# Head of a spectral-mixing block with its gradients: turned copies of grad_out and of the spectrum by DMA, the gate on w_down, inverse written in rows

## The chip, the cores and the metric

The kernel runs on one core of one Trainium2 chip. The core has five engines with a queue of instructions each: TensorE (PE, whose weight loads the profile lists as PEld), VectorE (DVE), ScalarE (ACT), GpSimd (POOL) and SyncE (SP, which issues most of the DMAs). Each engine takes its instructions in the order of its queue and waits on semaphores for what others make. The metric is the time of one execution on the device, in microseconds (us); lower is better.

## The reference

A block of a network with a modulated (adaLN) spectral filter and a modulated bilinear feed-forward part is run forward, and its gradients with respect to all inputs but one are formed for a given `grad_out`. x and grad_out are 1 x 2048 x 576 in bfloat16; w_gate and w_up are 576 x 4608, w_down 4608 x 576, w_mod 576 x 3456. Cut to what matters:

```python
mod = silu(c) @ w_mod                      # six vectors of 576: sa, ca, ga, sb, cb, gb
h = layernorm(x) * (1 + ca) + sa
x = x + ga * irfft2(rfft2(h) * (w_r + 1j * w_i))
h = layernorm(x) * (1 + cb) + sb
out = x + gb * (((h @ w_gate) * (h @ w_up)) @ w_down)
out, vjp = jax.vjp(f, A_x, A_w_r, A_w_i, B_w_gate, B_w_up, B_w_down, c, w_mod)
return out, *vjp(grad_out)
```

The gradient that reaches the hidden layer is `(gb * grad_out) @ w_down.T`. It does not depend on the forward pass, except on the vector gb.

## The kernel before, in words

The 2048 tokens lie on 128 partitions as 16 tiles (`NT`), token p*16+t in tile t. The 2-D Fourier transform is done by matmuls with tables: along the 576 columns to 289 frequencies (padded to 292, `FP`), then along the tokens in two steps, 16 x 128, with the twiddles in the tables. The frequencies are worked on in 73 groups of 4 (`NG`), and these in 19 chunks of 4 groups (`NCH`). F = 4608 is cut into 36 blocks of 128 (`NFB`).

The kernel has a head, a main loop over the 36 blocks (forward and gradient products of the feed-forward part: gup on line 581, u8p on line 607, u57p on line 526), and a tail (the way back through the norms and the filter). The change is in the head, which has these parts:

- The modulation vectors. `mod_load` (237) loads a sixth of w_mod, `mod_make` (243) multiplies and spreads it over all partitions as `modh[j]`, with the evacuation on DVE, and stores it. MSA comes first, then MCA; MGB (the gate gb) is made after the first `s1_cols`, the other three after stage 1.
- Stage 1, a software pipeline over 16 tiles: `s1_norm` (280) normalises a tile, modulates it and turns it on PE (trp), `s1_cols` (302) multiplies with the table RD (zp, evacuated into zt: the first half by ACT, the second by DVE), `s1_rows` (313) with G1 (vp) and writes the spectrum `VA`. x is loaded four tiles at a time by `x_load` (256), with the statistics of all four in one call of `norm_stats`.
- Stage 2, a pipeline over 19 chunks: `s2_turn` (343) turns four 128x128 blocks of VA on PE and ACT copies them out as VT; `s2_filter` (351) multiplies with BD2 (xp), ACT writes Xc, DVE multiplies with the filter (fm) and forms Yg; `s2_back` (369) turns Yg on PE, and DVE writes YT; `s2_inv` (377) multiplies with BDA (ap_), and ACT writes the result over the same columns of VA, with each frequency's 32 values (c, a) next to one another.
- Stage 3, a pipeline over 16 tiles: `s3_rows` (395) reads VA as weights, 128 frequencies with a stride of 32 elements, and goes back along the tokens; `s3_cols` (407) goes back along the columns with IR; `s3_norm` (421) forms x1 and the modulated h2, and every fourth tile's h2 is turned by a DMA into h2T (444).
- The product of the hidden gradient, called u4 (449 to 477): each tile of grad_out (gon) is multiplied by the gate on DVE (452) and turned on PE, five blocks a tile, into goT (458). Then w_down is loaded in 18 pairs of blocks (466), each pair is turned by a DMA into wdT (467; two buffers), and 720 matmuls of 128x512 (475) make ghhT, which is evacuated as ghh_st (two buffers; the first nine blocks on DVE, the rest by turns on ACT and DVE) and stored to DRAM (477). The main loop reads it from there.

u4 stands last in the program, but the compiler's scheduler writes one order for each engine and fills PE's gaps in stages 1 to 3 with u4's matmuls. `issue_after(x)` lets a DMA be issued only after instruction x; `high_priority` draws instructions forward. Within a queue nothing overtakes. SP's queue holds nearly all loads, all turns by DMA and the stores of the head. The tiles come from pools; a pool with n buffers makes the n+1st tile wait for the last reader of the first.

The gon product is used twice more: as the weights of u57p in the main loop, and as the rows of an output.

Of the kernel before, what the change touches and what calls it, by code (L numbers as in the profile page):

```python
# [82 lines left out]
def build(ctx, tc, A_x, A_w_r, A_w_i, B_w_gate, B_w_up, B_w_down, c_in, w_mod, grad_out,  # L83
# [39 lines left out]
    ones_f = glob.tile([128, 128], FP32, name="ones_f")  # L123
    nc.vector.memset(ones_f[:], 1.0)

    pick = glob.tile([128, 2, 128], BF, name="pick")
    nc.vector.memset(pick[:], 0.0)
    for q in range(2):
        nc.vector.memset(pick[:, q, 64 * q:64 * q + 64], 1.0)


# [11 lines left out]
    def norm_stats(xt, pool, nt, name, rstd_out):  # L143

        st = pool.tile([128, nt, 2, nc.vector.BN_STATS_DIM], FP32, name=name + "_st")
        mv = pool.tile([128, nt, nc.vector.BN_AGGR_DIM], FP32, name=name + "_mv")
        for t in range(nt):
            for h in range(2):
                nc.vector.bn_stats(out=st[:, t, h, :], in_=xt[:, t, h * 288:(h + 1) * 288])
            nc.vector.bn_aggr(out=mv[:, t, :], in_=st[:, t, :, :])  # L150
        nc.scalar.activation(out=rstd_out, in_=mv[:, :, 1], func=ACT.Sqrt, bias=eps_t[:], scale=1.0)
        nc.vector.reciprocal(out=rstd_out, in_=rstd_out)
        nmr = pool.tile([128, nt], FP32, name=name + "_nmr")
        nc.vector.scalar_tensor_tensor(out=nmr[:], in0=mv[:, :, 0], scalar=-1.0, in1=rstd_out, op0=MUL, op1=MUL)
        return nmr
# [28 lines left out]
    gonf = res2.tile([128, NT * D + 64], BF, name="gon")  # L184
    gon = gonf[:, 0:NT * D].rearrange("p (t d) -> p t d", t=NT)

    with ExitStack() as hs:
# [13 lines left out]
        r2 = hs.enter_context(ExitStack())  # L201
        r1 = r2.enter_context(ExitStack())
        wn = pool("hwn", 1, "right", stack=r2).tile([128, 2, NT, FP], BF, name="wn")
        hw2 = pool("hc1", 2, "right", stack=r1)
        modh = [hp1.tile([128, D], BF, name="modh%d" % j) for j in range(6)]
# [4 lines left out]
        nc.gpsimd.memset(gonf[:, NT * D:NT * D + 64], 0.0)  # L210
# [4 lines left out]
        c_bf = hp1.tile([128, 5], BF, name="c_bf")  # L215
        nc.vector.memset(c_bf[:], 0.0)
        with nc.allow_non_contiguous_dma(reason="tiny c load"):
# [25 lines left out]
        def mod_make(j, wm):  # L243
            for h in range(2):
# [5 lines left out]
                else:  # L250
                    evac(modh[j][:, h * 288:(h + 1) * 288], ps[:, 0:288], eng="v")
# [4 lines left out]
        def x_load(c4):  # L256
            xt = hw2.tile([128, 4, D], BF, name="xt", bufs=3)
            nc.sync.dma_start(xt[:], x_v[:, 4 * c4:4 * c4 + 4, :])
            xts.append(xt)

        wms = {MSA: mod_load(MSA)}
        x_load(0)
        wms[MCA] = mod_load(MCA)
        T = {"RD": load_table(hp1, "RD", "tA")}
        T["G1"] = load_table(hp1, "G1", "tB")
        first = mod_make(MSA, wms[MSA])
        mod_make(MCA, wms[MCA])
        with tc.issue_after(first):
            x_load(1)
            wms[MGB] = mod_load(MGB)  # L270
            nc.sync.dma_start(gon, go_v)
# [5 lines left out]
        Vv = VA[:].rearrange("k (g t c f) -> k g t c f", g=NG, t=NT, c=2)  # L277
        hTs, zts, n1s = {}, {}, {}

        def s1_norm(t):  # L280
            c4, tt = t // 4, t % 4
            if tt == 0:
# [4 lines left out]
                n1s["nmr"] = norm_stats(xts[c4], hw2, 4, "ln1", rstd1g[:, t:t + 4])  # L287
            n1 = n1s[c4]
            nc.scalar.activation(out=n1[:, tt, :], in_=xts[c4][:, tt, :], func=ACT.Identity, bias=n1s["nmr"][:, tt:tt + 1], scale=rstd1g[:, t:t + 1])
            nm = hw2.tile([128, D], BF, name="nm")  # L290
# [11 lines left out]
        def s1_cols(t):  # L302
            zt = zts[t] = hw2.tile([128, 2, FP], BF, name="zt", bufs=3)
            for cc in range(2):
# [3 lines left out]
                evac(zt[:, cc, :], zp[:, :FP], eng=("a" if cc == 0 else "v"))  # L308
            if t == 0:
                with tc.issue_after(mm.ins):  # L310
                    mod_make(MGB, wms[MGB])

# [21 lines left out]
        r1.close()  # L334
        with ExitStack() as rc:
            c2 = pool("hc2", 2, "right", stack=rc)
            VTs, Ygs, YTs = {}, {}, {}
# [5 lines left out]
            def s2_turn(ci):  # L343
                g0, ng, f0, w = dims(ci)
                pt = fps.tile([128, 4, 128], BF, name="trv", tag="fp")
                for j in range(ng):
                    nc.tensor.transpose(pt[:, j, :], VA[:, (g0 + j) * 128:(g0 + j + 1) * 128], ident[:])
                VT = VTs[ci] = c2.tile([128, 4, 128], BF, name="VT")
                evac(VT[:, 0:ng, :], pt[:, 0:ng, :], eng="a")

            def s2_filter(ci):
                g0, ng, f0, w = dims(ci)
                xp = fps.tile([128, 4, 128], FP32, name="xp", tag="fp")
                for j in range(ng):
                    nc.tensor.matmul(xp[:, j, :], lhsT=VTs[ci][:, j, :], rhs=T["BD2"][:], start=True, stop=True)
# [21 lines left out]
            def s2_inv(ci):  # L377
# [4 lines left out]
                Ac = VA[:, g0 * 128:(g0 + ng) * 128].rearrange("k (j f e) -> k j e f", f=4, e=2 * NT)  # L382
                evac(Ac, ap_[:, 0:ng, :].rearrange("k j (e f) -> k j e f", f=4), eng="a")

            pipeline(NCH, [s2_turn, s2_filter, s2_back, s2_inv])
            T["GB"] = load_table(hp1, "GB", "tB")
            T["IR"] = load_table(hp1, "IR", "tA")
        r2.close()
# [3 lines left out]
        Av = VA[:].rearrange("k (f c a) -> k f c a", c=2, a=NT)  # L392
        uts, ybs = {}, {}

        def s3_rows(sa):
# [3 lines left out]
            for fc in range(3):  # L399
                f0 = FS[fc]  # L400
                o = upa[:, fc, :] if fc < 2 else upb[:, 0, :]
                nc.tensor.matmul(o, lhsT=Av[:, f0:f0 + 128, 0, sa], rhs=T["GB"][:, sa, 1:3, :].rearrange("k v s -> k (v s)"), start=True, stop=False)
                nc.tensor.matmul(o, lhsT=Av[:, f0:f0 + 128, 1, sa], rhs=T["GB"][:, sa, 0:2, :].rearrange("k v s -> k (v s)"), start=False, stop=True)
# [724 lines left out]
```

## Time and profile before

| | us |
|---|---|
| median of three runs | 1632.08 |
| lowest and highest | 1628.67, 1633.07 |
| the profiled execution | 1636.95 |
| its span (first to last instruction) | 1635.2 |
| its head, up to the first gup matmul | 293.5 |
| PE busy | 1566.0 |
| DVE busy | 1007.8 |
| ACT busy | 567.6 |
| mean granted PE clock | 0.987 of full |

The profile comes from one execution recorded by the hardware. A view of it gives busy time by engine; groups of instructions by source line, with `out<-in` the names of the tiles; the idle time ahead of them and what ended it ("releaser"); and a timeline. L475 is line 475 of the kernel. A row on SP marked SPq is the time that its queue took to issue a DMA, not the time of the transfer; the time to its landing is listed separately.

### The profile page before, as it was taken

What the parts mean: (1) busy time and instruction counts of PE and PEld (TensorE: products, weight loads), DVE (VectorE), ACT (ScalarE), POOL (GpSimd) and SP (SyncE); (2) the same over time, 40 slices, a digit from 0 to 9 for tenths busy, and PEclk for the clock granted to TensorE, in tenths of its full rate; (3) what the DMA queues carried; (4) which work ended last, traced back from release to release, by engine and by line L of the source; (5) the groups of instructions that cost most, each with busy time, mean ns of one, the idle gap of its engine ahead of it and who ended that gap; (6) DMA issues with size and microseconds to landing.
All of it is one profiled execution on the core that took longest, in us unless ns stands there. A gap on an engine that the chain in (4) does not pass through costs nothing.

```text
span 1635.2 us, 29989 instructions
## 1 busy us (share of the span) xinstructions
PE 1566.0 (96%) x11354; PEld 1066.1 (65%) x11354; DVE 1007.8 (62%) x2642; ACT 567.6 (35%) x1056; POOL 161.3 (10%) x266
## 2 busy tenths in 40 slices
PE   6999999999999999999999999999999879899997
PEld 4645544566767676666767676666766656677765
DVE  7878733566564747565564747565564764678645
ACT  5697522322222222222222222222222355565022
POOL 0101100101000010101010010101000001100232
PEclk9999999999999999999999999999999989999998
DMA  9866976586768586776767686876757786636674
GB/s 349 289 183 196 267 214 192 148 162 123 145 134 165 114 170 121 158 147 114 161 129 153 135 161 117 161 135 142 158 103 136 190 240 202 231 97 193 254 216 151
DMA packets 482242, 280.35 MB, mean 171 GB/s; under 512 B 404753, under 2 KB 449426, under 8 KB 481202
## 3 DMA queue, kind: packets, MB, share of 16 engines
q1 hardware_dynamic: 462098, 204.26, 55.1%
q0 software_dynamic: 20000, 74.19, 15.5%
q8 instruction: 88, 1.44, 0.4%
q14 instruction: 56, 0.46, 0.1%
HBM read 108.51 MB, written 82.31 MB: 117 GB/s over the span
## 4 chain that ended last, share of the span: by engine, by line
PE 74%; DMA 6%; DVE 4%; issue 2%; ACT 2%; SPq 0%; POOL 0%; ACTq 0%; DVEq 0%; POOLq 0%
PE u57p L526 25%; PE gup L581 19%; PE u8p L607 17%; PE u4p L475 6%; PE u3p L1028 3%; DMA Xn<-xn_d 2%; DMA n2c<-n_d 2%; DMA wdB<-in_B_w_down_dram 1%; PE yp L937 1%; DMA out_dram<-o 1%; PE zp L801 1%; DVE gwt L849 0%; ACT u L956 0%; DMA x1t<-x_d 0%; DVE fm L167 0%
## 5 line engine op out<-in xcount | busy, mean ns | idle before, releaser
L612 DVE TENSOR_TENSOR acc<-acc,u8p 128x288 f32<-128x288 f32 x1088 | 429.4, 450 | 352.5 <-PE u8p L607 351.2
L581 PE MATMUL gup<-h2T,wgu 128*128 128x512 bf16 x1440 | 433.1, 379 | 0.0
L607 PE MATMUL u8p<-wT,ggT 128*128 128x288 bf16 x1152 | 314.7, 286 | 4.4 <-DVE acc L612 4.4
L607 PE MATMUL u8p<-wT,guT 128*128 128x288 bf16 x1152 | 314.7, 286 | 0.0
L581 PEld LDWEIGHTS <-wgu 128*128 128x128 bf16 x1440 | 140.8, 98 | 96.7
L528 ACT CAST so<-u57p 128x288 bf16<-128x288 f32 x216 | 86.2, 399 | 326.9 <-PE u57p L526 325.0
L607 PEld LDWEIGHTS <-guT 128*128 128x128 bf16 x1152 | 112.8, 98 | 101.5 <-issue 4.8
L475 PE MATMUL u4p<-goT,wdT 128*128 128x512 bf16 x720 | 165.0, 379 | 1.4 <-ACT ghh_st L139 1.4
L582 ACT CAST gT<-gup 128x512 bf16<-128x512 f32 x144 | 84.4, 586 | 226.6 <-PE gup L581 226.6
L526 PE MATMUL u57p<-gon,hh_sf 128*128 128x288 bf16 x1152 | 150.0, 287 | 0.0
L582 ACT CAST uT<-gup 128x512 bf16<-128x512 f32 x144 | 84.4, 586 | 188.5 <-PE gup L581 186.7
L526 PE MATMUL u57p<-h2p,gu_sf 128*128 128x288 bf16 x1152 | 148.8, 286 | 0.0
L526 PE MATMUL u57p<-h2p,gg_sf 128*128 128x288 bf16 x1152 | 148.2, 286 | 0.0
L1028 PEld LDWEIGHTS <-hl 128*128 128x128 bf16 x1152 | 112.9, 99 | 41.0 <-issue 11.3
L526 PEld LDWEIGHTS <-hh_sf 128*128 128x128 bf16 x1152 | 113.1, 98 | 35.1
L607 PEld LDWEIGHTS <-ggT 128*128 128x128 bf16 x1152 | 112.9, 98 | 29.0
L526 PEld LDWEIGHTS <-gu_sf 128*128 128x128 bf16 x1152 | 112.7, 98 | 28.4
L526 PEld LDWEIGHTS <-gg_sf 128*128 128x128 bf16 x1152 | 112.5, 98 | 28.3
L475 PEld LDWEIGHTS <-wdT 128*128 128x128 bf16 x720 | 69.2, 98 | 74.7 <-issue 1.9
L141 DVE CAST ghh_st<-u4p 128x512 bf16<-128x512 f32 x90 | 61.8, 687 | 67.7 <-PE u4p L475 64.7
L1028 PE MATMUL u3p<-wdB,hl 128*128 128x288 bf16 x672 | 96.4, 291 | 6.6 <-DMA wdB<-in_B_w_down_dram 5.8
L586 POOL DMA_DIRECT2D hhT_d<-hhT x36 | 33.2, 922 | 602.4 <-DVE hhT L583 598.7
(355 smaller groups left out, 1682.6 us busy)
## 6 DMA issues: line engine op xcount, KB each, us to landing
ghhT_d<-ghh_st SPq DMA_DIRECT2D x36, 512.0 KB, 3.3
ghh<-ghhT_d POOLq DMA_DIRECT2D x36, 512.0 KB, 7.7
hhT_d<-hhT POOLq DMA_DIRECT2D x36, 512.0 KB, 6.6
hl<-hhT_d SPq DMA_DIRECT2D x32, 576.0 KB, 7.9
out_dram<-woT SPq DMA_DIRECT2D x72, 128.0 KB, 2.0
wdn<-in_B_w_down_dram SPq DMA_DIRECT2D x18, 288.0 KB, 3.4
out_dram<-so SPq DMA_DIRECT2D x36, 144.0 KB, 2.4
wgu<-in_B_w_up_dram POOLq DMA_DIRECT2D x18, 256.0 KB, 5.3
```

What stands on the lines that cost most here:

```text
L141: nc.vector.tensor_copy(dst, src)
L475: nc.tensor.matmul(pt[:], lhsT=wdT[:, j, m, :], rhs=goT[:, 4 * sb4:4 * sb4 + 4, m, :], start=(m == 0), stop=(m == 4))
L526: mm = nc.tensor.matmul(pw[:, 0:288], lhsT=sf[:, t, :], rhs=rhs_n[:, t, h * 288:(h + 1) * 288], start=(t == 0), stop=(t == NT - 1))
L528: nc.scalar.copy(so[:, h * 288:(h + 1) * 288], pw[:, 0:288])
L581: nc.tensor.matmul(pt[:], lhsT=wgu[:, wi_, m, jw * 128:(jw + 1) * 128], rhs=h2T[:, ts_, m, :], start=(m == 0), stop=(m == 4))
L582: nc.scalar.copy(dstT[:, ts_, :], pt[:])
L586: nc.gpsimd.dma_start(hhT_d[:, :, fb, :].rearrange("tp f x -> f tp x"), hhT[:].rearrange("f (tp ti) p -> f tp (ti p)", ti=2))
L607: nc.tensor.matmul(pu[:, 0:288], lhsT=l_, rhs=r_, start=(k == 0), stop=(k == len(mms) - 1))
L612: nc.vector.tensor_tensor(out=dst, in0=dst, in1=pu[:, 0:288], op=ADD)
L801: nc.tensor.matmul(zp[:, :FP], lhsT=gyTs[t][:, m, :], rhs=T["RD"][:, m, cc, :], start=(m == 0), stop=(m == 4))
L937: nc.tensor.matmul(yp[:, 0:288], lhsT=ut[:, fc, cc * 128:(cc + 1) * 128], rhs=T["IR"][:, fc, cc, h * 288:(h + 1) * 288], start=(k == 0), s ...
L1028: mm = nc.tensor.matmul(p2[:, 0:288], lhsT=hls[fb // 9][:, fb % 9, ti * 128:(ti + 1) * 128], rhs=(wdA[:, fb] if fb < 15 else wdB[:, fb - 1 ...
```

## The change

- grad_out is not multiplied before it is turned. Four DMA turns of four tiles each (20 blocks of 128x128) make goT straight from the loaded grad_out, issued in the stage 1 code after the first `s1_cols`; the 80 PE transposes and 16 evacuations go. The gate is put on w_down's pairs, on DVE, after their load and ahead of their turn. gon is still multiplied by the gate for its later uses, but after the last h2.
- `s2_turn` goes. Five DMA turns (16, 16, 16, 16 and 9 blocks) make one VT of all of VA between stages 1 and 2, issued after the turn of w_down's fourth pair. Stage 2 is a pipeline of three steps.
- w_down's pairs are loaded and turned up to seven pairs ahead (two buffers of one pool and five of another): pairs 0 and 1 in stage 1, 2 and 3 after it, 4 to 6 after the VT turns, then one for each pair used.
- `s2_inv` writes VA as rows: for each c and a, all frequencies next to one another. `s3_rows` reads its 128 frequencies without a stride.
- Start: x's first tile is loaded and normalised alone, then tiles 2 to 4; MCA is made before MSA, MSA's evacuation is on ACT; the load of c is drawn forward.
- Evacuations: the second half of zt goes to ACT for odd tiles; ghh_st of the first nine blocks goes from DVE to ACT.
- Constants ones_f and pick are made in the tail, on POOL. The tables GB and IR are loaded after the VT turns.

The diff, cut to its core:

```diff
-                n1s["nmr"] = norm_stats(xts[c4], hw2, 4, "ln1", rstd1g[:, t:t + 4])
+            if t == 0 or tt == (1 if c4 == 0 else 0):
+                n = 1 if t == 0 else 4 - tt
+                nmr = norm_stats(xts[c4][:, tt:tt + n, :], hw2, n, "ln1", rstd1g[:, t:t + n], 4)
...
-        first = mod_make(MSA, wms[MSA])
         mod_make(MCA, wms[MCA])
+        first = mod_make(MSA, wms[MSA], "a")
...
+        def turn_pair(k):
+            f0 = k * FB4
+            wdT = wdTs[k] = (u4w if k % 7 < 2 else u4r[0]).tile([128, FB4, 5, 128], BF, name="wdT")
+            wdn = wdn2[:, k % 2, :, :]
+            with tc.issue_after(first):
+                nc.sync.dma_start(wdn[:, :, 0:D], B_w_down[f0 * 128:(f0 + FB4) * 128, :].rearrange("(j f) d -> f j d", f=128))
+            nc.vector.tensor_tensor(out=wdn[:, :, 0:D], in0=wdn[:, :, 0:D], in1=modh[MGB][:].unsqueeze(1).to_broadcast([128, FB4, D]), op=MUL)
+            turns.append(nc.sync.dma_start_transpose(out=wdT[:].rearrange("q j m f -> q (j m) f"), in_=wdn.rearrange("f j d -> f (j d)")).ins)
...
-                evac(zt[:, cc, :], zp[:, :FP], eng=("a" if cc == 0 else "v"))
+                evac(zt[:, cc, :], zp[:, :FP], eng=("a" if cc == 0 or t % 2 else "v"))
             if t == 0:
                 with tc.issue_after(mm.ins):
                     mod_make(MGB, wms[MGB])
+                for k in range(2):
+                    turn_pair(k)
+                    for t0 in (8 * k, 8 * k + 4):
+                        nc.sync.dma_start_transpose(out=goT[:, t0:t0 + 4, :, :].rearrange("q t m p -> q (t m) p"), in_=gon[:, t0:t0 + 4, :].rearrange("p t d -> p (t d)"))
...
+        u4r = [pool("u4r", 5, "right")]
+        for k in range(2, 4):
+            turn_pair(k)
...
+            VT = pool("hvt", 1, "right", stack=rc).tile([128, NG, 128], BF, name="VT")
+            for g0 in range(0, NG, 16):
+                g1 = min(g0 + 16, NG)
+                with tc.issue_after(turns[3]):
+                    vt_made = nc.sync.dma_start_transpose(out=VT[:, g0:g1, :], in_=VA[:, g0 * 128:g1 * 128]).ins
+            for k in range(4, 7):
+                turn_pair(k)
...
-            def s2_turn(ci):
...
-                Ac = VA[:, g0 * 128:(g0 + ng) * 128].rearrange("k (j f e) -> k j e f", f=4, e=2 * NT)
+                Ac = VA[:].rearrange("k (e f) -> k e f", f=FP)[:, :, f0:f0 + w].rearrange("k e (j f) -> k j e f", f=4)
...
-            pipeline(NCH, [s2_turn, s2_filter, s2_back, s2_inv])
+            pipeline(NCH, [s2_filter, s2_back, s2_inv])
...
-                nc.tensor.matmul(o, lhsT=Av[:, f0:f0 + 128, 0, sa], rhs=T["GB"][:, sa, 1:3, :].rearrange("k v s -> k (v s)"), start=True, stop=False)
+                nc.tensor.matmul(o, lhsT=Av[:, 0, sa, f0:f0 + 128], rhs=T["GB"][:, sa, 1:3, :].rearrange("k v s -> k (v s)"), start=True, stop=False)
...
-                nc.vector.tensor_tensor(out=gon[:, t, :], in0=gon[:, t, :], in1=modh[MGB][:], op=MUL)
...
-                nc.tensor.transpose(pt[:, m, :], gonf[:, t * D + m * 128:t * D + (m + 1) * 128], ident[:])
-            evac(goT[:, t, :, :], pt[:])
...
-                    evac(st[:, 4 * sb4:4 * sb4 + 4, :], pt[:], eng=("v" if fb < 9 else None))
+                    evac(st[:, 4 * sb4:4 * sb4 + 4, :], pt[:], eng=("a" if fb < 9 else None))
...
+            if fb0 // FB4 + 7 < NFB // FB4:
+                turn_pair(fb0 // FB4 + 7)
+        with tc.issue_after(h2_made[-1]):
+            for t in range(NT):
+                nc.vector.tensor_tensor(out=gon[:, t, 0:D], in0=gon[:, t, 0:D], in1=modh[MGB][:], op=MUL)
```

## The prediction

> **What bounds the kernel now.** I read the share of each engine first, then the span in 40 slices. TensorE is busy in nine tenths or more of nearly every slice; the slices that are not full are the first and a few in the tail.
>
> ```profile
> PE   6999999999999999999999999999999879899997
> ACT  5697522322222222222222222222222355565022
> ```
>
> The change touches the head alone (before the first gup matmul at 293.5 us), about the first seven slices. There PE looks as full as elsewhere, but in the head its fullness says little: the product of w_down and grad_out (line 475) is filler, put wherever PE would idle. So I cut the head at its own borders and asked for busy time in each stretch. Columns: stretch, length, busy time and count of PE, weight loads, DVE, ACT, POOL, then granted clock, DMA share, GB/s.
>
> ```profile
> 22.30:63.80 41.50, 37.92 (x345) 27.22 (x344) 37.27 (x109) 32.58 (x66) 2.13 (x4) 1.00 0.92 304
> 63.80:71.20 7.40, 6.50 (x63) 4.89 (x61) 4.11 (x9) 2.32 (x4) 0.00 (x0) 1.00 0.98 342
> 71.20:132.50 61.30, 56.00 (x461) 30.31 (x459) 48.60 (x131) 57.81 (x56) 5.16 (x9) 1.00 0.64 198
> 132.50:186.50 54.00, 49.96 (x351) 34.09 (x351) 45.90 (x136) 35.84 (x74) 10.81 (x20) 1.00 0.82 230
> 186.50:293.50 107.00, 105.65 (x490) 47.74 (x489) 38.73 (x66) 31.94 (x55) 2.47 (x5) 1.00 0.75 213
> ```
>
> These are stage 1 (its first 22 us left out), the gap before the chunks, the 19 chunks of stage 2, stage 3, and the rest of the filler. In the chunks ACT is the fullest (57.81 of 61.30); the same view of line 475 alone puts 167 filler matmuls (42.28 us) there, 62 in stage 3 and 488 in the last stretch. So every piece of a stage that gets shorter saves nothing by itself: the filler not done in it is done after stage 3, at 0.216 us a matmul (405 of them in 87.57 us in one row of the timeline). What counts is when stage 3 ends, and how much filler is left then.
>
> The timeline shows one chunk, from one transpose of Yg to the next, 2.76 us (start, length, engine, line; the mean pace over 19 chunks is 61.3/19 = 3.2):
>
> ```profile
> 81.45 0.40 PE L373 MATMUL try__1011<-ident,Yg 128*128 128x128 bf16 x4 [0.17 <-DVE Yg L367]
> 81.69 0.39 PE L355 MATMUL xp<-T_BD,VT 128*128 128x128 bf16 x4
> ...
> 82.11 0.71 ACT L139 CAST Xc<-xp 128x512 bf16<-128x512 f32 x1
> ...
> 82.70 0.61 ACT L139 COPY VT<-trv 128x512 bf16<-128x512 bf16 x1
> ...
> 82.86 0.76 DVE L167 TENSOR_TENSOR fm<-Xc,wn 128x512 bf16<-128x512 bf16 x2 [0.53 <-ACT Xc L139]
> ...
> 83.17 2.46 ACT L139 CAST VA<-ap__1039 128x512 bf16<-128x512 f32 x1
> ...
> 83.86 0.29 DVE L367 TENSOR_TENSOR Yg<-fm 128x256 bf16<-128x256 bf16 x1
> ...
> 84.21 0.40 PE L373 MATMUL try__1045<-ident,Yg 128*128 128x128 bf16 x4 [0.18 <-DVE Yg L367]
> ```
>
> ACT needs 0.7 + 0.6 + 2.5 = 3.8 us at its longest; but the chain xp, Xc, fm, Yg, transpose alone takes 2.6 to 2.8 us with ACT prompt, as here, since each chunk's Yg comes behind the last one's.
>
> **The change, part by part.** The order in which each engine gets its instructions is fixed; I compared it before and after. In the main loop PE's order is the same; the tail differs in some 150 places without a new wait. I take both at zero, give or take 2.
>
> *PE transposes removed:* 73 of VA and 80 of grad_out. At spacings of 0.057 (four in 0.23 us) and 0.065 us (15 in about 1.0) that is 9 us of PE work. It is a gain only where PE does not idle instead.
>
> *Turns by DMA.* In their place come 4 turns of 20 blocks (grad_out) and 5 of 73 blocks in all (VA). What SP needs to issue one, in the rows of before:
>
> ```profile
> 44.78 7.99 SPq L467 DMA_TRANSPOSE wdT<-wdn  x2
> 153.39 3.06 SPq L444 DMA_TRANSPOSE h2T<-h2p  x1
> 375.44 2.25 SPq L591 DMA_TRANSPOSE gu_sf<-guT  x1
> 377.78 7.32 SPq L591 DMA_TRANSPOSE hh_sf<-hhT  x1
> 385.16 2.19 SPq L591 DMA_TRANSPOSE gg_sf<-ggT  x1
> ```
>
> These are 20, 20, 16, 16 and 16 blocks: 0.4, 0.15, 0.14, 0.46 and 0.14 us a block. Three stacked turns (48 blocks) land in 8.6 to 11.9 us, 0.18 to 0.25 a block. I take 0.18, and 0.136 and 0.4 as ends.
>
> *Stage 1.* In SP's new order the load of the last four x tiles stands behind 4 turns of grad_out and 2 of w_down (100 blocks), the first of which waits for grad_out (issued at 14.20, 12.7 us to landing: 26.9) and issues near 29. Before, the same x load was issued at 23.42 and landed 7.3 us later. Now: 29 + 100 x 0.18 = 47, landed about 52; DVE needs it at 45.3 by the pace of before. Stage 1 ends **6 us** later (2.5 at 0.136 a block, 12 at 0.25 and up; -2 if DVE, which loses 16 casts of zt to ACT at 0.46 each, makes the stage shorter and the load is in time). The loads of wr and wi, and of the last mod vectors, stand behind it as well. The split of x's first tile starts transposes some 1.5 us earlier, but MGB's matmuls still wait for their weights: 0.
>
> *Gap and stage 2.* The VA turns wait for the fourth w_down turn, which stands behind the modb stores, and those behind the mod evacuation. Before, that was done 8.0 us after stage 1's end; with a store and a turn issued after it I put the first VA turn at 9.8. ACT's first write into VA (chunk 0's inverse) must wait for all five turns, since they read all of VA, and it stands in ACT's queue ahead of the Xc of chunk 3: so the chunks can't pass the third until the last turn has landed, 73 x 0.18 + 1.8 = 15 (12 to 20) after the first's issue. From there 16 chunks at 2.7: ACT has lost VT (0.66) and writes VA in rows of f, for which the nearest rows are the tail's contiguous writes of A, median 0.603 and 0.586, against 2.43 to 2.60; so the chain of 2.6 to 2.8 binds, not ACT. With 3 us of drain: 9.8 + 15 + 16 x 2.7 + 3 = 71 against 68.7 from stage 1's end to the last chunk before (63.8 to 132.5): **+2.3** (-3 to +11). So the ACT relief, 19 x 0.5 = 9.5, is real and is eaten by the wait for VT; if that cover were gone the stage would gain it.
>
> *Idle PE and its clock.* While VA is turned PE has only 49 fillers (10.6 us) in some 25 us, and for chunks 1 to 8 none, since the next evacuation of filler stands on ACT behind chunk 9: its buffer waits for a store that stands deep in SP's queue. Before, an idle of 4.39 us on PE in the tail was followed by a clock of 0.76:
>
> ```profile
> 1399.74 1.12 PE L1028 MATMUL u3p<-wdB,hl 128*128 128x288 bf16 x4 [4.39 <-DMA wdB<-in_B_w_down_dram]
> ```
>
> and in the 10 us window after it the granted clock was 0.76, with four 128x128 matmuls at 0.107 apart rather than 0.057. **+2** (0, when the chain hides it, to 4.5). The Trainium skill, "TensorE: Matmul & The Clock Gate", section "HAM oscillation — how this bites in real kernels", has a rule that speaks against such a change: an idle window of about 3.4 us halves PE's clock and some 3.4 us of steady work brings it back; by it, chunks with PE a quarter busy might stay at half clock throughout, and 16 chunks with some 12 matmuls each at 0.05 us more would cost about 10 us (an estimate). The row shows the drop, but not how long a thin load holds it.
>
> *Stage 3 and the rest.* Stage 3 holds 56 fillers in place of 62 and does not begin behind a 2.5 us write of VA: **-2** (0 to -4). 513 fillers are left behind it in place of 488: 25 x 0.216 = **+5.4**. The gon multiplications move behind h2 on DVE (16 x 0.447), and two of DVE's evacuations may queue behind a burst: **+0.5** (0 to 1); ghh_st of the first nine blocks on ACT (0.586 rather than 0.687) covers the rest, as does u4p's buffering. The gate's product on a pair of w_down, not in the trace, is some 2 x 0.447 = 0.9 us on DVE by gon's row; DVE is busy 38.73 us of the last 107, which hides 11 of the 18, and the two in stage 1 stand ahead of its zt casts, at 1.8 if nothing covers them, which the x wait does. The memsets moved to the tail run on POOL (10% busy): 0.
>
> Sum: 6 + 2.3 + 2 - 2 + 5.4 + 0.5 = **+14** on the profiled execution's 1636.95 (span 1635.2), so 1651 for such an execution; against the median, 1632.1 + 14 = **1646**. That execution is 0.3% over the median, about what a measurement of this kernel can tell from no change.
>
> **The rivals.** (a) *The turns are hidden and PE work counts.* If the DMA turns land before anyone needs them and the filler fills the gaps, the 9 us of transposes is all that is left: 1632 - 9 = 1623, and up to 1627 by the terms below. For it: PE is 96% busy. Against it: VA can't be turned before stage 1 ends, and only 49 fillers stand there. It decides if the last VA turn lands within 16 us of stage 1's end, for then stage 2 is 71 - 8.8 = 62, 6.5 shorter, and x in time (-2) with no cold clock: -2 - 6.5 - 2 + 5.4 + 0.5 = -5, down to -9 when the filler goes where the idle is. (b) *Quick turns*, 0.136 a block: x 2.5 late, VT 12, no cold clock: 2.5 - 0.7 - 2 + 5.4 + 0.5 = +5.7, and with x in time as well (-2 for the 2.5) +1.2: 1633 to 1638, mostly within 0.3%. (c) *Turns in contention*: stage 1's DMA share is 0.92 already; at 0.25 and more, x is 12 late, VT takes 20, the clock costs 4.5, and the mod loads are late too: 12 + 7.3 + 4.5 + 5.4 + 1 = +30: 1662. (d) *The change does not do what it says*, transposes being still there: no, the order has 306 PE rows fewer (153 loads, 153 matmuls).
>
> **How the numbers follow.** Forecast (1637 to 1655) 0.53; (a) 0.13; (b) 0.17; (c) 0.17. Faster by over 0.3% (under 1627.2) is (a), 0.13; within is (b), 0.17; slower (over 1637.0) is forecast and (c), 0.70. The range 1627 to 1662 leaves out (a) and the upper part of (c), 2 in 10 in all.
>
> **What would show it.** In the profile after: the x load of line 258's successor issued near 47 and DVE idle on it; stage 1 ending near 70; the first VA turn some 10 us later, PE idle with VT as the releaser, and a clock under 0.9 there; ACT's write of VA near 0.6 us and the chunk pace near 2.7; stage 3 ending near 195 in place of 186.5, and the first gup near 307. It is wrong if the turns issue at 0.14 a block or less and PE never idles, or if the chunks, free of ACT's 2.5 us, run well under 2.6 us.

## The result and the profile after

The changed kernel takes 1670.95 us, the median of four runs (1669.57 to 1671.89), against 1631.55 before (four runs, 1628.67 to 1633.07): 39.4 us more, a ratio of 1.0243 with a 95% interval of 1.0225 to 1.0261. The prediction said 1646, range 1627 to 1662: the right direction, and 25 us short. The profiled execution took 1671.89 us with a span of 1670.1.

The page's slices, after:

```profile
PE   6759979999999999999999999999999999899997
ACT  5536722232222222222222222222222265466122
PEclk9969989999999999999999999999999999999999
```

A slice is 41.8 us long. Where PE was full from the second slice on, now the second, third and sixth have gaps, and the granted clock has fallen in the third and, less, in the sixth. The same cut into stages as in the prediction (stage 1, the gap, the chunks, stage 3, the rest of the filler; columns as there):

```profile
23.50:78.00 54.50, 42.33 (x313) 27.68 (x311) 29.92 (x80) 35.11 (x72) 2.13 (x4) 0.94 1.02 297
78.00:92.10 14.10, 12.79 (x74) 6.79 (x72) 3.21 (x7) 4.60 (x9) 0.00 (x0) 1.00 0.76 179
92.10:155.70 63.60, 42.36 (x305) 23.86 (x306) 36.39 (x103) 29.89 (x55) 0.52 (x1) 0.73 0.88 223
155.70:208.00 52.30, 48.53 (x345) 32.15 (x345) 43.05 (x129) 36.34 (x77) 10.81 (x20) 1.00 0.78 229
208.00:337.60 129.60, 114.04 (x516) 50.84 (x515) 49.50 (x90) 33.46 (x58) 7.07 (x13) 0.96 0.63 178
```

Three places stand out. Stage 1 ends at 78.0 and not 63.7, with the DMA engines at 1.02 of their time. The chunks run at a clock of 0.73, with ACT idle over half the time. The last stretch takes 129.6 us where PE is busy for 114. The first gup is at 337.6: 44.1 us later than before. The span grew by 34.9, so 9 us came back behind the head, where the change hardly touches anything. Of those, 5 are the old profiled execution, that much over its median; from first gup to end the runs below whose tail is the old one take 1331.5 to 1339.1 us, the old execution 1341.6. So the head carries the whole loss.

Two of the things that DVE waited for in the head, after (us in total, times, longest; its waits for PE and ACT are left out):

```profile
DVE wdn L281 <- DMA wdn<-in_B_w_down_dram: 36.6, 12, 10.8
DVE ln_st L140 <- DMA xt<-in_A_x_dram: 7.9, 3, 4.7
```

The first row is a wait that the kernel before does not have: the gate's product on a pair of w_down, in DVE's queue, waits for the load of that pair.

### The profile page after: what moved, and what is told of

Same layout as the page of the kernel before. It is cut to its first block, busy times and chain, and to the rows that moved or that the text cites. A ratio compares the mean times of both kernels' runs of the same rounds, so it can differ in the third digit from the quotient of the medians.

```text
span 1670.1 us, 29700 instructions
## 1 busy us (share of the span) xinstructions
PE 1566.8 (94%) x11201; PEld 1061.8 (64%) x11201; DVE 995.7 (60%) x2604; ACT 548.1 (33%) x1077; POOL 162.6 (10%) x270
## 4 chain that ended last, share of the span: by engine, by line
PE 76%; DMA 7%; DVE 6%; ACT 2%; issue 1%; SPq 1%; ACTq 0%; DVEq 0%
PE u57p L529 24%; PE gup L584 18%; PE u8p L610 16%; PE u3p L1038 7%; PE u4p L473 6%; DMA n2c<-n_d 2%; DMA wdn<-in_B_w_down_dram 1%; DMA wdB<-in_B_w_down_dram 1%; PE yp L947 1%; DMA wdT<-wdn 1%; SPq L553 1%; ACT u L966 1%; DVE fm L158 1%; PE zp L811 1%; DVE acc L615 1%
## 5 line engine op out<-in xcount | busy, mean ns | idle before, releaser
L473 PE MATMUL u4p<-goT,wdT 128*128 128x512 bf16 x720 | 170.4, 386 | 17.8 <-DVE ghh_st L132 13.4
L130 ACT CAST ghh_st<-u4p 128x512 bf16<-128x512 f32 x90 | 52.5, 587 | 106.1 <-PE u4p L473 83.9
```

The lines of the kernel that those rows point to most:

```text
L130: nc.scalar.copy(dst, src)
L473: nc.tensor.matmul(pt[:], lhsT=wdT[:, j, m, :], rhs=goT[:, 4 * sb4:4 * sb4 + 4, m, :], start=(m == 0), stop=(m == 4))
```

## The experiments

Two lists of theories were tried: what delays (VectorE's queue held by the gate, SyncE's queue, VA's turn), and, when undoing these one by one gave little back, what each part costs when it is put alone into the kernel before. "Filler" is a matmul of u4, 0.216 us each. Times are medians, with the kernel before measured on the same chip beside them; "+" is against that. Where stages matter, I give stage 1's end / stage 3's end / first gup from the profile (before: 63.7 / 186.4 / 293.5; after: 78.0 / 208.0 / 337.6), and the filler done ahead of stage 3's end (before 232, after 207).

**Undoing one thing in the changed kernel.**

The gate's product on GpSimd.

```diff
-            nc.vector.tensor_tensor(out=wdn[:, :, 0:D], in0=wdn[:, :, 0:D], ...
+            nc.gpsimd.tensor_tensor(out=wdn[:, :, 0:D], in0=wdn[:, :, 0:D], ...
```

> The changed kernel with one edit: the gate's product on w_down's pairs is done by GpSimd and no longer by VectorE. Theory Q (the load that the product waits for holds VectorE's queue: 36.6 us of such waits stand in the head, 3.1, 1.6 and 4.2 of them inside stage 1, 3.0 in the chunks, 10.8 and 5.4 behind stage 3): the waits move to GpSimd, stage 1 ends some 9 us earlier (near 69.5 rather than 78.5), the chunks lose 3 to 5 more, and the whole lands at 1650 to 1658. Rival S (what is late is SyncE's queue: x, stores and mod weights stand behind the turns, and VectorE only shows it): the time stays within 4 us of 1671.

Measured 1671.75, +40.6 (75.4 / 227.4 / 343.7). No gain; but the run is no clean test, since GpSimd's product takes 2.37 us and stops DVE (the last section), and POOL's stores now stand behind the wait for w_down.

The load of x ahead of the turns.

```diff
-            if t == 0:
...
+            if t == 4:
                 for k in range(2):
                     turn_pair(k)
```

> The changed kernel with one edit: the turns of grad_out and of w_down's first two pairs are put behind the load of x's last four tiles in the program (after the fifth tile's columns, not the first's), so that this load is issued ahead of them. Theory S (SyncE's queue): the wait of 4.7 us for x on VectorE goes, stage 1 ends 5 us or more earlier, 1662 to 1666. Theory Q (VectorE's queue held by the gate's product): the product's waits grow by what x no longer hides, since w_down's loads are no earlier: within 4 us of 1671.

Measured 1676.96, +45.8 (80.7 / 213.6 / 343.0). DVE's wait for x fell from 7.9 to 3.1, its waits for w_down rose from 36.6 to 40.9. With x in time stage 1 ends no earlier: what one load gains, the next loses, and the place of x's load in the queue is not the limit by itself.

The spectrum turned on PE again, with the old inverse.

```diff
-                    vt_made = nc.sync.dma_start_transpose(out=VT[:, g0:g1, :], in_=VA[:, g0 * 128:g1 * 128]).ins
+            def s2_turn(ci):
...
-            pipeline(NCH, [s2_filter, s2_back, s2_inv])
+            pipeline(NCH, [s2_turn, s2_filter, s2_back, s2_inv])
```

> The changed kernel with the spectrum turned on TensorE again, chunk by chunk with ScalarE's copy, and the inverse written as before (the rows can't be written over what is not yet turned). Theory V (waiting for VA's turn, and the half clock from 97 to 130 us, is the main loss): stage 2 takes 62 from the end of stage 1's gap as before, clock 1.00 there, and the time falls by 12 or more, to under 1659. Theory Q: VectorE's waits for w_down stay; the gain is what stage 2 lost, 7 us less what filler fits, 1664 to 1668.

Measured 1669.28, +38.1 (79.5 / 213.0 / 334.4). The chunks did not become faster, 69 us from first to last xp: ACT has VA's old write, VT's copy and now also the casts of filler, and is busy 68.5 of these 69 us.

The gate on grad_out, ahead of its turn.

```diff
-            nc.vector.tensor_tensor(out=wdn[:, :, 0:D], ...
+                for t_ in range(NT):
+                    nc.vector.tensor_tensor(out=gon[:, t_, 0:D], in0=gon[:, t_, 0:D], in1=modh[MGB][:], op=MUL)
```

> The changed kernel with the gate put on grad_out again, ahead of its turn by DMA (16 products of 0.447 us on VectorE in stage 1), and none on w_down. Theory Q: no VectorE instruction waits for w_down any more; 1650 to 1658, like the run with the product on GpSimd, less some microseconds for the 16 products standing in stage 1 and the turns of grad_out starting later. Theory S: the turns stand as before ahead of x's load, and later: 1671 or more.

Measured 1666.42, +35.3 (81.0 / 212.6 / 328.9): some 4 us back, where the theory of the gate's waits forecast 13 or more, and stage 1 ends no earlier.

Both turns on PE, the gate on grad_out, the old inverse; the new start, the pairs ahead and the casts on ACT stay.

```diff
-                        nc.sync.dma_start_transpose(out=goT[:, t0:t0 + 4, :, :].rearrange("q t m p -> q (t m) p"), ...
+                nc.tensor.transpose(pt[:, m, :], gon[:, t, m * 128:(m + 1) * 128], ident[:])
...
-                    vt_made = nc.sync.dma_start_transpose(out=VT[:, g0:g1, :], ...
+                    nc.tensor.transpose(pt[:, j, :], VA[:, (g0 + j) * 128:(g0 + j + 1) * 128], ident[:])
```

> The changed kernel with both turns on TensorE again, the gate on grad_out, and the inverse as before; what remains of the change is the start, the seven pairs ahead and the moved evacuations. Theory F: nearly all of the loss is gone, 1630 to 1638. If the seven pairs ahead were a main cause (their loads and turns ahead of the chunks' stores on SyncE): 1645 or more.

Measured 1663.93, +32.1 (66.3 / 207.3 / 329.5). Without a single turn of grad_out or VA 32 us remain; but that is no price of the turns, for this run has a loss of its own that the changed kernel has not. Stage 1 is on time again; ACT is busy all of 80 to 140 us (60.00 of 60), since the casts of filler came to it and the cheaper write of VA was taken from it; and PE is idle for 12.8 us behind stage 3. The two runs below that have these things alone, the casts on ACT with VA's old write (+20.6) and the pairs ahead (+14.8), come to about as much.

Pairs two ahead, all else as changed, and the casts of filler on DVE, all else as changed:

```diff
-            wdT = wdTs[k] = (u4w if k % 7 < 2 else u4r[0]).tile(...)
+            wdT = wdTs[k] = u4w.tile(...)
```

> The changed kernel with w_down's pairs two ahead as before, and nothing else undone. PE's order has 164 fillers ahead of stage 3; the changed kernel had 150 in its trace. Theory A: the stores and loads come in time, the idle of 16 us behind stage 3 goes and 1671 becomes 1645 to 1655. Theory G: 14 fillers, 3 us: 1664 to 1670.

```diff
-                    evac(st[:, 4 * sb4:4 * sb4 + 4, :], pt[:], eng=("a" if fb < 9 else None))
+                    evac(st[:, 4 * sb4:4 * sb4 + 4, :], pt[:], eng=("v" if fb < 9 else None))
```

> The changed kernel with the casts of the first nine blocks' filler (ghh_st) on VectorE again. PE's order has 181 fillers ahead of stage 3, against 150 in the changed kernel's trace. Theory G: 31 x 0.216 = 6.7 us less, and PE warm in more of the chunks, another 3: 1658 to 1665. Theory A: the waits for stores and loads are as before, and take back what the order gains: 1667 to 1674.

Measured 1666.24 (+36.0; 78.9 / 205.9 / 326.6) and 1670.55 (+40.3; 78.4 / 216.7 / 337.7). The first gives back 3 to 5 us. The second kept 37 fillers more ahead of stage 3's end, and stage 3 ended 8.7 us later: filler moved is not time gained.

**One part alone in the kernel before.**

72 blocks turned by DMA that nobody reads.

```diff
+            if t == 4:
+                for k in range(4):
+                    nc.sync.dma_start_transpose(out=h2T[:].rearrange("q t m p -> q (t m) p")[:, 18 * k:18 * k + 18, :], in_=T["RD"][:].rearrange("p a b c -> p (a b c)")[:, 0:2304])
```

> The kernel before with one addition: in stage 1, behind the load of x's last tiles, four DMA turns of 18 blocks each (72 blocks of the table RD) into h2T, which nobody reads and stage 3 writes over. Theory F (a turn costs the DMA engines' time, by the queue's rows 26 us of all 16 engines for 153 blocks, 0.17 each, in a stretch where they were 0.92 busy): the loads behind come later, stage 1 or the gap ends 6 to 12 us later, 1637 to 1644 in all. Theory W (only the waits cost that the change itself adds, on VectorE for w_down and on ScalarE for VA's turn): within 3 us of 1631.

Measured 1640.82, ratio 1.006 (1.004 to 1.0079), +9.0. Stage 1 ends at 64.7, but the first chunk comes at 83.7 instead of 72.3, since the weights of MCB, loaded later, are late (PE waited 8.1 us for them). Issuing the four turns held SP's queue for 17.7 us, 0.25 a block, and the first chunk came 11.4 us later.

VA turned by DMA and the inverse in rows.

```diff
+            for g0 in range(0, NG, 16):
+                g1 = min(g0 + 16, NG)
+                nc.sync.dma_start_transpose(out=VT[:, g0:g1, :], in_=VA[:, g0 * 128:g1 * 128])
...
-            pipeline(NCH, [s2_turn, s2_filter, s2_back, s2_inv])
+            pipeline(NCH, [s2_filter, s2_back, s2_inv])
```

> The kernel before with this part of the change alone: VA turned by five DMAs into one VT after stage 1, and the inverse written in rows; grad_out, the gate, w_down's pairs and the start are as before. Theory F: 73 blocks cost about half of the whole, 1645 to 1652, most of it between stage 1's end and the first chunks. Theory W: the wait for VT is paid (some 12 us) but ScalarE's relief, 19 times 2.5 less 0.6 us and VT's copies, gives it back where VectorE doesn't wait for w_down: 1630 to 1638.

Measured 1630.16, ratio 0.999 (0.9973 to 1.0006): no loss (63.9 / 204.9 / 297.5). Stage 3 ends 18.5 us later, but 298 fillers are done by then, 66 more than before, 14.3 us of work. PE in this run waited only here for the turns (ACT's first write into VA waited 2.0 us):

```profile
PE xp L351 <- DMA VT<-VA: 1.4, 1, 1.4
```

The inverse in rows alone, into an array of its own.

```diff
-                Ac = VA[:, g0 * 128:(g0 + ng) * 128].rearrange("k (j f e) -> k j e f", f=4, e=2 * NT)
+                Ac = VB[:].rearrange("k (e f) -> k e f", f=FP)[:, :, f0:f0 + w].rearrange("k e (j f) -> k j e f", f=4)
```

> The kernel before with the inverse written in rows, into an array of its own, and nothing else: ScalarE's write of a chunk falls from 2.5 to about 0.6 us. By both theories this is a gain that the change paid for: the chunks go from 3.2 to about 2.8 us each, of which the filler that no longer fits is done later; PE's idle time in stage 2 (61.3 less 56.0 us busy) bounds it: 1626 to 1631.

Measured 1636.53, ratio 1.0034 (1.0017 to 1.005). Stage 3 ends at 178.7, 7.7 us earlier, yet first gup is at 295.0: PE waited 8.5 us behind stage 3. The new array holds 18.7 KB a partition to the end of the head. That was the hint to look at memory.

The seven pairs ahead alone (with the filter's array wn kept to the end of the head, as the change keeps it).

```diff
-            wdT = u4w.tile([128, FB4, 5, 128], BF, name="wdT")
+            wdT = wdTs[k] = (u4w if k % 7 < 2 else u4r[0]).tile([128, FB4, 5, 128], BF, name="wdT")
...
-        r2.close()
```

> The kernel before with w_down's pairs loaded and turned seven ahead and nothing else (no gate on them; the filter's array stays allocated through the head, since the five more buffers lie above it). PE's order has as many fillers ahead of stage 3 as before, 171. Theory A (the loads and turns ahead stand in SyncE's queue in front of the stores of the chunks and of ghhT, and the main loop's first loads come later for the memory): 1642 to 1656, with waits for ghhT's stores on ScalarE and VectorE. Theory G (what costs is the filler moved out of the first stages by the order, and the gate's waits): 1629 to 1637.

Measured 1645.11, ratio 1.0094 (1.0077 to 1.011), +14.8 (63.6 / 184.2 / 312.0). Stage 3 ends earlier than before, with the same 232 fillers; the whole loss lies behind it, 127.8 us for 488 fillers that took 107.1. The waits of ACT in that stretch:

```profile
ACT ghh_st L139 <- PE u4p L484: 59.0, 37, 2.9
ACT ghh_st L139 <- DMA ghhT_d<-ghh_st: 35.1, 6, 15.5
```

ACT waited 15.5 us for one buffer of ghh_st, whose block was not yet stored, and no filler can run while both buffers are full.

The memory alone: nothing turned ahead, the filter's array and 12.8 KB a partition kept allocated.

```diff
-        r2 = hs.enter_context(ExitStack())
...
         r1.close()
+        kept = pool("kept", 1, "right").tile([128, 5 * 2 * 5 * 128], BF, name="kept")
...
-        r2.close()
```

> The kernel before, with the memory of the filter's array and 12.8 KB beside it kept allocated to the end of the head, as the five more buffers keep it, and nothing turned ahead. Theory M (behind stage 3 the loss of the seven pairs ahead is that the main loop's first loads have no memory until stage 3 ends, and then fall together with the last turn of h2 and hold the stores of ghhT, 12 to 15 us to landing): the first wgu load moves from 72 to about 190 us, PE idles 8 us or more behind stage 3, and the time is 1640 to 1650, like the run with the pairs ahead alone (1645). Rival (the turns ahead fill SyncE's queue themselves): 1629 to 1634.

Measured 1645.52, ratio 1.0092 (1.0067 to 1.0117), +13.4 (62.7 / 184.2 / 304.1): the loss of the pairs ahead, without the pairs. The timeline of this run behind stage 3, and PE's wait there:

```profile
193.09 4.86 SPq L444 DMA_TRANSPOSE h2T<-h2p  x1
...
193.52 0.76 POOL L563 DMA_DIRECT2D wgu<-in_B_w_up_dram  x1
...
194.79 1.10 POOL L570 DMA_DIRECT2D ghh<-ghhT_d  x2
...
198.04 9.74 SPq L467 DMA_TRANSPOSE wdT<-wdn  x1
...
207.88 0.54 SPq L477 DMA_DIRECT2D ghhT_d<-ghh_st  x1
...
214.09 1.07 ACT L139 CAST ghh_st<-u4p 128x512 bf16<-128x512 f32 x2 [14.99 <-DMA ghhT_d<-ghh_st]
```

```profile
PE u4p L475 <- ACT ghh_st L139: 12.2, 2, 11.9
```

The tiles of the main loop's first weights (wgu) and of ghh lie over memory of the head. In the kernel before, wgu was loaded from 71.9 us on, and the issue of w_down's turn behind the last turn of h2 was short:

```profile
71.87 0.77 POOL L563 DMA_DIRECT2D wgu<-in_B_w_up_dram  x1
...
200.56 1.36 SPq L467 DMA_TRANSPOSE wdT<-wdn  x1
```

Now wgu's memory comes free with stage 3, and the load goes out at 193.52, beside the last turn of h2. That turn takes 18.5 us to landing, where the four of the kernel before took 6.5 to 8.8, and the issue of the next turn of w_down holds SyncE's queue for 9.74 us in place of 1.36. The store of ghhT behind it goes out at 207.88, and ACT has its buffer at 214.09.

All twenty traces sort themselves by this. Take the time from stage 3's end to the first gup, less 0.216 us for each filler left: it is 0 to 4 us in the nine runs that free the head's memory as before (the kernel before among them; wgu is first loaded well ahead of stage 3's end), and 11 to 22 us in the eleven that keep some of it (the changed kernel: 18.8; wgu is loaded with stage 3's end or after it).

The casts of filler on ACT alone.

```diff
-                    evac(st[:, 4 * sb4:4 * sb4 + 4, :], pt[:], eng=("v" if fb < 9 else None))
+                    evac(st[:, 4 * sb4:4 * sb4 + 4, :], pt[:], eng=("a" if fb < 9 else None))
```

> The kernel before with the casts of the first nine blocks' filler on ScalarE and nothing else; ScalarE was busy 57.81 of 61.30 us in the chunks. PE's order has 142 fillers ahead of stage 3 against 171. Theory G: 29 x 0.216 = 6 us more behind stage 3 and chunks slower by ScalarE's extra casts: 1638 to 1648. If the filler only moves into idle time elsewhere: 1630 to 1634.

Measured 1650.85, +20.6 (65.1 / 204.1 / 311.3): with the old write of VA (2.5 us) ACT is the limit of the chunks, which take 67.5 us in place of 57.8 from first to last xp, with ACT busy 67.0 of them.

**Building the change up.** grad_out by DMA alone (gate on it ahead of the turn, spectrum on PE, memory freed; the change's new start and its split of zt's evacuations come along in these four runs and have no run of their own); then with VA's turn and the rows; then the last with one thing more. Against the kernel before:

```diff
-                nc.tensor.transpose(pt[:, m, :], gonf[:, t * D + m * 128:t * D + (m + 1) * 128], ident[:])
+                        nc.sync.dma_start_transpose(out=goT[:, t0:t0 + 4, :, :].rearrange("q t m p -> q (t m) p"), in_=gon[:, t0:t0 + 4, :].rearrange("p t d -> p (t d)"))
```

> Of the change only the turn of grad_out by DMA and the new start: the gate on grad_out ahead of the turn, the spectrum on TensorE, the inverse as before, pairs two ahead, the casts on VectorE, memory freed as before. PE's order has 207 fillers ahead of stage 3. Theory T (80 blocks in stage 1's full DMA queues make it late, 64 to 79 us in every run that has them): stage 1 ends at 75 to 81; 1640 to 1650. If stage 1's lateness came from the gate on w_down: stage 1 ends at 64 to 68 and 1627 to 1634.

Measured 1637.52, ratio 1.0038 (1.0023 to 1.0054), +5.4 (80.5 / 209.9 / 304.5). Stage 1's lateness comes with the turn of grad_out: it ends at 75 to 82 us in all eleven runs that turn it by DMA, the changed kernel among them, and at 62 to 67 in all nine that do not, the kernel before among them, and one with the new start. But late is not lost: 288 fillers ran ahead of stage 3's end.

```diff
-            pipeline(NCH, [s2_turn, s2_filter, s2_back, s2_inv])
+                    vt_made = nc.sync.dma_start_transpose(out=VT[:, g0:g1, :], in_=VA[:, g0 * 128:g1 * 128]).ins
+            pipeline(NCH, [s2_filter, s2_back, s2_inv])
```

> Both turns by DMA and the inverse in rows, with the new start, but the gate on grad_out, pairs two ahead, the casts on VectorE and memory freed as before. PE's order has 217 fillers ahead of stage 3. By theories T and M together the loss behind stage 3 is gone and that of stage 1 stays, the turn of VA is neutral as alone: 1640 to 1650. If the two turns make each other worse (DMA time): 1655 or more.

Measured 1645.67, ratio 1.0087 (1.0061 to 1.0114), +13.5 (81.8 / 216.5 / 312.5). Together the two turns cost some 10 us more than the sum of the two alone (+5.4 and -1.6); by the intervals of the three runs that is 10, give or take 6.

```diff
-                for t_ in range(NT):
-                    nc.vector.tensor_tensor(out=gon[:, t_, 0:D], ...
+            nc.vector.tensor_tensor(out=wdn[:, :, 0:D], ...
```

> Both turns by DMA bare (1645.7, with the gate on grad_out, pairs two ahead, the casts on VectorE, memory freed), and one thing of the change put back: the gate's product on w_down's pairs on VectorE. PE's order has 205 fillers ahead of stage 3 against 217. If VectorE's waits for w_down's loads (36 us in the changed kernel) cost by themselves: 1653 to 1660. If they are only another name for the late queue, as the run with the product on GpSimd suggests: 1643 to 1649.

Measured 1657.67, ratio 1.017 (1.0144 to 1.0197), +26.9 (81.8 / 218.6 / 321.4): 13.4 more than bare. Its waits:

```profile
DVE wdn L282 <- DMA wdn<-in_B_w_down_dram: 30.7, 13, 7.4
DVE ln_st L140 <- DMA xt<-in_A_x_dram: 6.7, 3, 4.0
```

```diff
-                    evac(..., eng=("v" if fb < 9 else None))
+                    evac(..., eng=("a" if fb < 9 else None))
```

> Both turns by DMA bare (1645.7), and one thing of the change put back: the casts of the first nine blocks' filler on ScalarE. PE's order has 185 fillers ahead of stage 3 against 217: 32 x 0.216 = 7 us more behind stage 3, if no time is saved ahead of it: 1650 to 1656. If the stages get shorter by the fillers that they no longer hold: 1643 to 1649.

Measured 1642.25, ratio 1.0065 (1.0047 to 1.0083), +11.5: 2 less than bare, which is within the noise of the two. With the cheaper write of VA, ACT has room for the casts; they add nothing.

**The part that costs nothing, and one step more.** VA by DMA and rows, with stage 3's rows of x asked for two steps earlier.

```diff
+            if sa % 2 == 0:
+                xcs[sa // 2] = hw2.tile([128, 2, D], BF, name="xc")
+                nc.sync.dma_start(xcs[sa // 2][:], x_v[:, sa:sa + 2, :])
```

> The run with VA's turn by DMA and the inverse in rows alone, with one thing more: stage 3 asks for its rows of x (xc) two steps earlier, so that the load is not behind the main loop's first loads (VectorE waited 4.0 us for it, PE 3.5, and then ran at a clock of 0.66 for 10 us). If that stall counts: 4 to 6 us under 1630, 1623 to 1627. If filler moves only: 1629 to 1631.

Measured 1631.08, ratio 0.9999 (0.9984 to 1.0014). No gain: DVE's wait for xc is still 3.6 us. No version here beats the kernel before by a measurable amount.

**The account.** Against the kernel before: both turns bare, with the new start, 13.5; the gate on w_down 13.4 more; the casts -2.0; the memory, by the pairs ahead alone, 14.8. The sum is 39.7, and the change measured 39.4. So near a fit is luck: each part is known to 3 to 6 us, and the parts are not independent, as the undoings show. The gate moved off w_down gives back some 4 and not 13.4 while the memory is held. Two pairs ahead give back 3 to 5 and not 15; that run still keeps the filter's array, and its first wgu load is at 214.6 us.

## Why the prediction was wrong

**Right, by its own steps.** The last x load was put at an issue of 47 and landing at 52: 48.54, and DVE went on at 53.90. The first turn of VA was put 9.8 us after stage 1: 9.6 (87.57). The five turns were put at 15 us: ACT's first write of VA waited for them until 101.0, 13.4 after the first issue. ACT's write fell to 0.58 as said. 513 fillers were left behind stage 3, as said. Stage 3 itself: 52.3 for 53.9, for a forecast of -2. Chunk and clock show in ACT's rows of the changed kernel, two chunks at half clock and two at full clock:

```profile
108.97 0.58 ACT L130 CAST Xc<-xp 128x512 bf16<-128x512 f32 x1 [2.01 <-issue]
...
112.05 0.58 ACT L130 CAST Xc<-xp 128x512 bf16<-128x512 f32 x1 [1.84 <-DVE YT L132]
...
145.58 0.58 ACT L130 CAST Xc<-xp 128x512 bf16<-128x512 f32 x1
...
148.24 0.59 ACT L130 CAST Xc<-xp 128x512 bf16<-128x512 f32 x1 [0.74 <-PE xp L371]
```

3.08 us from Xc to Xc at half clock and 2.66 at full clock, for the 2.7 predicted. The clock fell for long:

```profile
100.00:128.00 28.00, 12.19 (x86) 8.16 (x87) 13.75 (x39) 9.72 (x18) 0.00 (x0) 0.50 1.01 249
128.00:136.00 8.00, 7.90 (x53) 4.45 (x51) 5.21 (x14) 5.40 (x11) 0.00 (x0) 0.80 0.71 206
```

28 us at 0.50, with PE busy 44% of them, and back when filler made PE busy all the time. That is nine chunks at 0.42 more, 3.8 us, inside the range of 0 to 4.5. The prediction's rule from the Trainium skill, "TensorE: Matmul & The Clock Gate" (its windows of 3.4 us stand in the section "🔬 Part 1: The HAM clock gate (the "warmup" mystery)"), is borne out in one half: the thin load did not bring the clock back, and some 4 us of unbroken matmuls did (127.3 to 131). The other half, that it takes an idle window of 3.4 us to lose the clock, is not: it fell at 97 us, when PE's longest idle stretch since 78 us was 1.3 us. And the 10 us that the prediction estimated by the rule were too many. Most of what the chunks lost beyond the clock is one step from Xc to Xc of 7.74 us (98.15 to 105.89), in which DVE waited 3.0 us for a pair of w_down and ACT 3.8 for a store of Xc, which stood behind the turns of VA in SP's queue.

**Wrong, three terms.** By stages the 44.1 are: stage 1 +14.3 (predicted 6), the gap and chunks +8.9 (2.3 and 2 for the clock), stage 3 -1.6, behind it +22.5 (5.9).

*Behind stage 3* is the step that failed most, 16.6 us. The prediction priced the last stretch by its fillers alone, and the seven pairs ahead at nothing: it has no term for them. It took the pairs ahead for a matter of when they are turned, and did not ask which later load needs the memory that their buffers and the filter's array keep. The order of POOL's queue, where the wgu loads stand behind the last stores of stage 3, told it and was not read. What the runs showed in its place: with that memory kept and nothing else changed, 13.4 us. In the changed kernel:

```profile
219.95 4.71 SPq L460 DMA_TRANSPOSE h2T<-h2p  x1
224.70 1.01 SPq L280 DMA_DIRECT2D wdn<-in_B_w_down_dram  x1
225.82 0.76 SPq L475 DMA_DIRECT2D ghhT_d<-ghh_st  x1
...
228.29 9.78 SPq L282 DMA_TRANSPOSE wdT<-wdn  x1
```

```profile
239.00 16.57 PE L473 MATMUL u4p<-goT,wdT 128*128 128x512 bf16 x65 [10.34 <-DVE ghh_st L132]
```

The same picture as with the memory held alone: the first wgu load goes out at 220.0, a store of ghhT and a load of w_down issued at 225 land at 237 to 238, the next turn's issue takes 9.78 us, and PE idles 10.34. That the kept memory is the cause was shown by its own run; that the transfers are slow because so much is under way at once is only read from these rows, and no run took one of them away.

*The gate on w_down* was counted as 0.9 us a product, "hidden" behind the last 107 us or covered by the x wait. Its length was right (0.76 us); that it waits in DVE's queue for a load was left out. By the build-up it costs 13.4 us, give or take 6.

*Stage 1* was priced by the x load alone. x was late as said, but four products of the gate stood in stage 1, not two, and three of them waited (3.1, 1.6 and 4.2 us). Either wait is enough by itself: with x in time (the run with x first) two products waited 7.6 and 4.1 us and stage 1 ended at 80.7; with no such product (the turn of grad_out alone) DVE waited 7.0 us for x and it ended at 80.5. The prediction also left out that filler now runs inside stage 1: 25 to 31 matmuls, 5 to 7 us of PE, in each of the eleven runs with the turn (26 in the changed kernel), and none in the nine without it. That part is work moved forward and no loss. How the rest of the 14.3 divides is not settled.

Of the rivals, (b) fell with the late x and the cold clock. (a) found no support: VA's turn alone takes some 4 of the 9 us from PE, with a cheaper write of VA besides, and the time stays. (c), 1662, came nearest in size, for the wrong reason: the turns issued at 0.15 a block for VA and 0.19 for grad_out (8.26 + 6.91 us for 80), not at 0.25. What stays open is why the two turns together cost more than the sum of each alone. The traces show two things: the fillers done ahead of stage 3's end, which pay for a late stage, are 288 and 298 with one turn and 293 with both; and the clock is at 0.50 for 17 us of the chunks with both, for 3 us with VA's alone and never with grad_out's alone. A shared limit of the DMA engines (1.02 of their time in the changed kernel's stage 1, 1.01 from 100 to 128 us) is possible and was not tested by taking load away.

## What to carry to other kernels

Ask of each new buffer whose memory it keeps and which later load was waiting for that memory: the price of a deeper prefetch can be the prefetch of the next phase. A cheap instruction put into an engine's queue costs the wait for its operand, for everything behind it too; look for the load's landing, not for the instruction's length. And where filler closes gaps, judge a stage by its end and its fillers together: VA's turn alone made stage 3 end 18.5 us later and cost nothing.

## What the runs showed of the hardware

A GpSimd product stops VectorE's operations on two arrays. In the run with the gate's product on GpSimd, one of DVE's subtractions and additions of two arrays, 0.28 us elsewhere, took as long as the GpSimd product beside it:

```profile
111.78 0.29 DVE L382 TENSOR_TENSOR Yg<-fm 128x256 bf16<-128x256 bf16 x1
111.92 2.37 POOL L281 TENSOR_TENSOR wdn<-wdn,modh 128x1152 bf16<-128x1152 bf16 x1 [6.95 <-DMA wdn<-in_B_w_down_dram]
111.99 2.44 DVE L383 TENSOR_TENSOR Yg<-fm 128x256 bf16<-128x256 bf16 x1
```

The product itself, 0.76 us on DVE, takes 2.37 on GpSimd. DVE's casts and copies of one array beside it kept their 0.4 to 0.7 us. The Trainium skill, "SBUF — State Buffer", section "🔬 SBUF: two separate sides", says that the two engines share a pair of ports, and that either a GpSimd operation or a DVE operation with two inputs in SBUF holds it for a whole instruction while the other waits; the rows agree, and the run with the gate on GpSimd could not tell what it was made for.
